# Query maxima of 12 of 32 attention units carried by an accumulating DMA, with a new order table: a hand-ordered attention and feed-forward kernel

## Chip, cores and metric

The kernel runs on one core of a Trainium2 chip. The metric is device time in microseconds (us). The engines are PE (matrix products), DVE (VectorE), ACT (ScalarE), POOL (GpSimd) and SP (SyncE, which here issues most DMAs).

## The reference

The reference is a kernelised attention over 8 batches × 8 heads, sequence 576, head dimension 64, 128 features, and a feed-forward block with a cosine behind it:

```
def phi(x):
    proj = np.einsum('bhsd,df->bhsf', x, w_phi)
    proj = proj - np.max(np.abs(proj), axis=-1, keepdims=True)
    return np.concatenate([np.exp(proj), np.exp(-proj)], axis=-1)
q_p, k_p = phi(q), phi(k)
kv  = np.einsum('bhsf,bhsd->bhfd', k_p, v)
z   = np.sum(k_p, axis=2)
num = np.einsum('bhsf,bhfd->bhsd', q_p, kv)
den = np.einsum('bhsf,bhf->bhs', q_p, z)[..., None] + 1e-06
attn_out = num / den

x = attn_out as (4608, 512)
h = x @ w_in            # 512 x 2048
g = h * np.cos(h)
out = g @ w_out         # 2048 x 512
```

The step the change is about is `proj - max|proj|` for the queries: every token has one maximum over the 128 features.

## The kernel before

The host hands over `q` and `k` transposed, two heads to a unit, so there are 32 units. For each, `attention(u)` writes down the steps of its work; `convert` and `fold` write down the preparation of `w_in` and `w_out`, `visit` the feed-forward block for single blocks of tokens, `visit_two` for two blocks together. Nothing is issued while these functions run. Each piece is a `Step` with its engine, a cost, what it depends on and which buffers it takes and uses. `plan()` (L260) then walks one hand-kept list, `ORDER` (L88), of 3852 step numbers, assigns PSUM banks and the two value buffers, and the steps are issued in that order. So each engine works strictly in the order in which its steps stand in the list, and so does SP's queue of DMA issues: a load that waits for a buffer holds up every load behind it.

Projections of a unit's queries have the feature index on the 128 partitions and the 2 × 576 tokens along the free axis, in `pq` (ACT copies them there from PSUM, `q_copy`, L583). The maximum over partitions is made in these steps:

- `q_red` (DVE, L589): a reduction with transposition inside blocks of 32×32 gives `m1`, with absolute values taken.
- `q_max` (DVE, L597, L598): the four groups of 32 partitions are brought down to one, `m3`.
- `q_spread` (POOL, L603): three copies put it back on the other three groups.
- `q_turn` (DVE, L607): a transposition of 128×1152 spreads every maximum over the partitions, into `bq`.
- `q_sub` (POOL, L611): four subtractions `pq - bq`, a quarter of the tokens each.
- `exp_q` (ACT, L682): the exponentials into `eq`, from which PE computes the numerators and denominators (`x_mm`, L755).

The keys have tokens on partitions, so that DVE takes their maximum directly (`k_max`, L656; `k_neg`, L659) and ACT subtracts it as a bias in the exponential (`exp_k`, L676). PE forms `kv` (L722, L728), ACT copies it (`kv_out`, L734), DVE divides (L767 to L785), SP stores the result to DRAM, `xs` and `xs_tail`.

In the feed-forward part `hi_of` and `lo_of` (L50 on ACT, L55 on DVE) split a tile into a rounded part and a rest, so that a product is three matmuls: L1023 to L1025 in `visit`, L1374 to L1376 in `visit_two`. `x` comes back by loads `x_raw<-xs` (L1116), parts and sums of `w_out` by `wo<-wo_parts` (L1351) and `wo<-wo_sums` (L1347), all on SP. The cosine waves are L981 to L1007 and L1296 to L1307, each an alternation of DVE and ACT. L398 to L423 are conversions of `w_in` and `w_out` on DVE.

Attention, conversions and the `visit`s share the first 535 us; the three `visit_two` fill the rest. The value buffers and the place of every step are set here:

```
elif b.ring == "v":
    b.slot, n_v = n_v, 1 - n_v
return [steps[i] for i in ORDER]
```

Of the kernel before, what the change touches and what calls it, by code (L numbers as in the profile page):

```python
# [17 lines left out]
P = 128  # L18
# [8 lines left out]
def phi_attention_then_cos_ffn(ctx: ExitStack, tc: tile.TileContext, qkT, vS, w_phi, w_in, w_out, out, out_t):  # L27
# [41 lines left out]
    class Step:  # L69
# [190 lines left out]
    def plan():  # L260
        place = {steps[x]: i for i, x in enumerate(ORDER)}
        owner = [None] * len(banks)
        n_v = 0

        def last(b):
            return -1 if b is None else max(place[v] for v in b.users)

        for x in (steps[i] for i in ORDER):
            for b in x.take:
# [4 lines left out]
                elif b.ring == "v":  # L274
                    b.slot, n_v = n_v, 1 - n_v
# [1318 lines left out]
```

## Time and profile before

| | |
|---|---|
| runs | 1010.91, 1015.84, 1015.05 us; median 1015.05 |
| profiled execution | 1013.98 us, its span 1012.3 us, 22252 instructions |
| mean granted clock of PE | 0.998 |
| busy | PE 991.7 us (98%), DVE 892.5 (88%), ACT 769.7 (76%), POOL 164.3 (16%) |
| DMA | 210.60 MB, mean 208 GB/s |
| chain that ended last, by engine | PE 77%, DVE 10%, DMA 7%, ACT 2%, issue 2%, POOL 1% |

The span is what the profiler recorded from the first instruction to the last; the profiled execution's own time is 1.7 us longer. Busy time is the time in which an engine has an instruction in work. A share of the whole span mixes stretches in which different engines are full, so the table is only where one begins. In rows of the trace, `PEclk` is TensorE's granted clock as a share of full speed, `SPq` is SP's queue, and an arrow in brackets names what ended an engine's idle time.

### The profile page before, as it was taken

How to read it: one execution, taken by the hardware profiler on the slowest of the kernel's cores; microseconds unless marked ns; L12 is line 12 of the kernel's file. 1: busy time of each engine (PE TensorE's matmuls, PEld its weight loads, DVE VectorE, ACT ScalarE, POOL GpSimd, SP SyncE). 2: the span in 40 equal slices, each digit the busy share in tenths (PEclk: the TensorE clock that was granted, in tenths of full speed). 3: DMA queues.
4: the chain of work that ended last, by engine and by line, in shares of the span. 5: the costliest groups of instructions: out<-in, count | busy, mean ns of one | idle time of the engine just before them, and what ended most of it. 6: DMA issues, size and time to landing. Idle time of an engine off the chain costs nothing.

```text
span 1012.3 us, 22252 instructions
## 1 busy us (share of the span) xinstructions
PE 991.7 (98%) x8586; PEld 803.5 (79%) x8586; DVE 892.5 (88%) x1590; ACT 769.7 (76%) x1575; POOL 164.3 (16%) x231
## 2 busy tenths in 40 slices
PE   9999999999999999999989999899999999999997
PEld 6778878888788878788767888688888888888886
DVE  6999999999899999899989979798778998787984
ACT  6899999688878988899997666557565766665653
POOL 4544130121112123333550000000000000000000
PEclk9999999999999999999999999999999999999999
DMA  6667776456676578888767663447546575375364
GB/s 233 187 192 229 240 214 206 138 188 233 208 236 205 212 227 286 282 283 254 232 198 247 222 217 141 158 165 270 200 151 228 171 219 206 126 247 203 98 225 145
DMA packets 104569, 210.60 MB, mean 208 GB/s; under 512 B 21392, under 2 KB 52240, under 8 KB 100880
## 3 DMA queue, kind: packets, MB, share of 16 engines
q1 hardware_dynamic: 104320, 209.13, 62.4%
q8 instruction: 67, 1.10, 0.4%
q14 instruction: 38, 0.31, 0.1%
q10 hardware_dynamic: 144, 0.07, 0.0%
HBM read 152.54 MB, written 56.62 MB: 207 GB/s over the span
## 4 chain that ended last, share of the span: by engine, by line
PE 77%; DVE 10%; DMA 7%; ACT 2%; issue 2%; POOL 1%; SPq 1%; DVEq 0%; POOLq 0%; ACTq 0%
PE bank L1201 23%; PE bank L974 9%; PE bank L1374 7%; PE bank L1376 7%; PE bank L1375 7%; PE bank L1023 3%; PE bank L1025 3%; PE bank L1024 3%; PE bank L755 3%; PE bank L722 3%; PE bank L618 2%; PE bank L572 2%; DMA vs<-vS 1%; DVE mk L656 1%; DVE m L589 1%
## 5 line engine op out<-in xcount | busy, mean ns | idle before, releaser
L1374 PE MATMUL bank<-gh,wo 128*128 128x512 f32 x336 | 132.4, 394 | 6.0 <-DMA wo<-wo_parts 4.2
L676 ACT ACTIVATE ek<-bank,mk 128x128 f32<-128x128 f32 x464 | 132.9, 486 | 4.2 <-DVE mk L659 2.3
L611 POOL TENSOR_TENSOR pq<-pq,bq 128x288 f32<-128x288 f32 x128 | 120.1, 969 | 97.9 <-DVE bq L607 72.0
L1376 PE MATMUL bank<-gl,wo 128*128 128x512 f32 x336 | 132.0, 393 | 0.0
L1375 PE MATMUL bank<-gh,wo 128*128 128x512 f32 x336 | 131.7, 392 | 0.0
L682 ACT ACTIVATE eq<-pq 128x576 f32<-128x576 f32 x128 | 83.8, 793 | 6.2 <-POOL pq L611 4.8
L603 POOL COPY m<-m 32x36 f32<-32x36 f32 x96 | 43.4, 452 | 268.3 <-DVE m L598 254.2
L1298 ACT ACTIVATE g<-hs 128x512 int32<-128x512 f32 x96 | 59.6, 626 | 34.7 <-DVE hs L1217 33.6
L1304 ACT ACTIVATE g<-g,halfpi 128x512 f32<-128x512 f32 x96 | 66.9, 717 | 24.8 <-DVE g L1301 24.6
L1201 PE MATMUL bank<-x_eq,wi 128*128 128x512 f32 x216 | 84.8, 393 | 0.1
L1211 ACT ACTIVATE hs<-bank 128x512 f32<-128x512 f32 x96 | 56.0, 591 | 35.6 <-PE bank L1201 25.2
L1374 PEld LDWEIGHTS bank<-gh,wo 128*128 128x128 f32 x336 | 63.4, 189 | 21.5 <-issue 6.7
L1023 PE MATMUL bank<-wo,gh 128*128 128x512 f32 x192 | 77.2, 402 | 0.6 <-ACT pq L583 0.4
L1201 PE MATMUL bank<-xh_t,wi 128*128 128x512 f32 x192 | 76.0, 396 | 0.3 <-ACT hs L1211 0.3
L1025 PE MATMUL bank<-wo,gl 128*128 128x512 f32 x192 | 75.3, 392 | 0.3 <-DVE gl L55 0.2
L1024 PE MATMUL bank<-wo,gh 128*128 128x512 f32 x192 | 74.9, 390 | 0.0
L1376 PEld LDWEIGHTS bank<-gl,wo 128*128 128x128 f32 x336 | 63.5, 189 | 14.2
L1301 DVE SCALAR_TENSOR_TENSOR g<-g,hs 128x512 f32<-128x512 int32 x96 | 64.9, 686 | 11.1 <-ACT g L1298 10.8
L1375 PEld LDWEIGHTS bank<-gh,wo 128*128 128x128 f32 x336 | 63.6, 189 | 13.8
L755 PEld LDWEIGHTS bank<-kv,eq 128*64 128x64 f32 x2048 | 64.9, 138 | 11.8 <-issue 3.4
L755 PE MATMUL bank<-kv,eq 128*64 128x65 f32 x2048 | 70.8, 223 | 1.3 <-DVE rb L781 0.5
L722 PE MATMUL bank<-vs,ek 128*64 128x65 f32 x2048 | 67.4, 223 | 1.9 <-ACT ek L676 1.5
(170 smaller groups left out, 2517.2 us busy)
## 6 DMA issues: line engine op xcount, KB each, us to landing
wi<-wi_parts SPq DMA_DIRECT2D x18, 1792.0 KB, 7.6
wo<-wo_sums SPq DMA_DIRECT2D x20, 1024.0 KB, 6.1
qk<-qkT SPq DMA_DIRECT2D x31, 640.0 KB, 5.3
x_raw<-xs SPq DMA_DIRECT2D x47, 256.0 KB, 4.0
wo<-wo_parts SPq DMA_DIRECT2D x22, 512.0 KB, 8.8
vs<-vS SPq DMA_DIRECT2D x32, 325.0 KB, 4.9
wi_raw<-w_in SPq DMA_DIRECT2D x8, 1024.0 KB, 6.3
wo_raw<-w_out SPq DMA_DIRECT2D x8, 1024.0 KB, 6.6
```

The source lines that it names most:

```text
L611: qeng.tensor_tensor(out=d["pq"][:, c], in0=d["pq"][:, c], in1=d["bq"][:, c], op=ALU.subtract)
L676: ACT.activation(out=e[:, g, s * P:(s + 1) * P], in_=pk[:, g, :], func=AF.Exp, scale=1.0 - 2.0 * s, bias=d["lk" if s == 0 else "mk", i][:, ...
L722: PE.matmul(out=acc[c:c + 64, n, i, :], lhsT=e[:, s, P * n + c:P * n + c + 64], rhs=vs[b["v"].slot][:, 2 * s + i, :], start=(s == 0 and i ...
L755: PE.matmul(out=ps[64 * h:64 * h + 64, 65 * t:65 * t + 65], lhsT=d["eq", i][:, n, c:c + 64], rhs=d["kv"][:, 2 * n + i, :], start=h not in ...
L974: PE.matmul(out=bank(b), lhsT=w[:, part, 2 * r + kt // 2, kt % 2 * P:(kt % 2 + 1) * P], rhs=d.get(("from", kt), d)[x, kt], start=(k == 0), ...
L1023: PE.matmul(out=a, lhsT=gh[:, t], rhs=w[:, 0, r], start=first, stop=False)
L1024: PE.matmul(out=a, lhsT=gh[:, t], rhs=w[:, 1, r], start=False, stop=False)
L1025: PE.matmul(out=a, lhsT=gl[:, t], rhs=w[:, 0, r], start=False, stop=last)
L1201: PE.matmul(out=bank(bank_b), lhsT=w[:, part, block, j * P:(j + 1) * P], rhs=d[x, name, j], start=start and k == 0, stop=k == 5, skip_grou ...
L1374: PE.matmul(out=a, lhsT=w_of(0, m), rhs=n["gh"], start=first, stop=False, skip_group_check=True)
L1375: PE.matmul(out=a, lhsT=w_of(1, m), rhs=n["gh"], start=False, stop=False, skip_group_check=True)
L1376: PE.matmul(out=a, lhsT=w_of(0, m), rhs=n["gl"], start=False, stop=True, skip_group_check=True)
```

## The change

For units 10 to 21 the query maxima take another way. `q_red` writes the negated maxima, with the tokens of a block read side by side. `q_least` takes minima of them into a constant tile `least` of 32×64 and transposes it into `m4`, in which a partition holds the 32 tokens of a block. `q_put` writes `m4` to DRAM as one row of 1152 numbers, `most_q[u]`. `q_add` reads that row for all 128 partitions at once and adds it to `pq` in the DMA itself (`accum_op=ALU.add`). Both DMAs are issued by POOL. `q_spread`, `q_turn` and the four `q_sub` do not exist for these units; the other 20 units keep them. Value buffers go to the one that is freed first in the order, instead of alternating. `ORDER` is written anew: 3804 numbers in place of 3852. DVE has 12 steps fewer, POOL 36 fewer; PE, ACT and SP have as many as before.

```diff
     def plan():
         place = {steps[x]: i for i, x in enumerate(ORDER)}
         owner = [None] * len(banks)
-        n_v = 0
+        owner_v = [None] * len(vs)
...
                 elif b.ring == "v":
-                    b.slot, n_v = n_v, 1 - n_v
+                    b.slot = min(range(len(vs)), key=lambda i: last(owner_v[i]))
+                    assert last(owner_v[b.slot]) < place[x]
+                    owner_v[b.slot] = b
...
+    least = const.tile([32, 64], F32, name="least")
+    POOL.memset(least, 0.0)
...
+    Q_ADDED = range(10, 22)
...
+    most_q = dram.tile([NU, 2, 2 * NJ, 32], F32, name="most_q")
...
         def q_red(j):
+            if u in Q_ADDED:
+                DVE.tensor_reduce(out=d["m1"][:, 2 * j * NJ:2 * (j + 1) * NJ],
+                                  in_=d["pq"][:, j * S:(j + 1) * S].rearrange("p (b f) -> p b f", f=32), axis=AX.X,
+                                  op=ALU.max, apply_absolute_value=True, apply_transpose=True, negate=True)
+                return
...
+        def q_least():
+            m1 = d["m1"]
+            m2 = new("bq", [64, 4 * NJ], F32, "m2", "m2")
+            d["m4"] = new("bq", [32, 64], F32, "m4", "m4")
+            DVE.tensor_tensor(out=m2, in0=m1[0:64], in1=m1[64:128], op=ALU.min)
+            DVE.tensor_tensor(out=least.rearrange("p (j c) -> p j c", j=2)[:, :, 0:2 * NJ],
+                              in0=m2[0:32].rearrange("p (j c) -> p j c", j=2), in1=m2[32:64].rearrange("p (j c) -> p j c", j=2), op=ALU.min)
+            DVE.transpose(out=d["m4"], in_=least)
+        def q_put():
+            POOL.dma_start(out=most_q[u].rearrange("h j t -> j h t"), in_=d["m4"][0:2 * NJ].rearrange("j (h t) -> j h t", h=2))
+        def q_add():
+            most = most_q[u].rearrange("h j t -> (h j t)").unsqueeze(0).broadcast_to([P, 2 * S])
+            POOL.dma_start(out=d["pq"], in_=most, accum_op=ALU.add)
...
-        qm = Step("DVE", 0.41, q_max, reds, take=[b["bq"]], use=[b["pq"]], port=True, kind=phase + "q_max")
...
+        if u in Q_ADDED:
+            qm = Step("DVE", 0.58, q_least, reds, take=[b["bq"]], use=[b["pq"]], port=True, kind=phase + "q_max")
+            qm = Step("POOL", 0.9, q_put, [qm], use=[b["bq"]], kind=phase + "q_put")
+            qs = [Step("POOL", 0.9, q_add, [qm], use=[b["pq"]], kind=phase + "q_add")] * 4
+        else:
+            qm = Step("DVE", 0.41, q_max, reds, take=[b["bq"]], use=[b["pq"]], port=True, kind=phase + "q_max")
...
             eqs.append(Step("ACT", 1.15, lambda j=j: exp_q(j),
-                            qs[2 * j:2 * j + 2], take=[e], use=[b["pq"]],
+                            qs[2 * j:2 * j + 1] if u in Q_ADDED else qs[2 * j:2 * j + 2], take=[e], use=[b["pq"]],
...
     ORDER = [
-        0, 3, 42, 4, 5, 59, 7, 45, 44, 1, 6, 8, 9, 17, 18, 10, 19, 46, 21, 11, 48, 58, 1265, 47, 12, 62, 14, 23, 20, 22, 15, 2, 49, 25,
...
```

The order table moves steps everywhere. Three places matter for what follows. Lines behind the edit have moved: L1116, L1351 and L1347 before are L1145, L1380 and L1376 now; L50 and L55 stay; L676, L682 and L1004 are L705, L711 and L1033. In the rows, a name's number tells one buffer from the next, `x4` is a count of equal instructions.

The first place is SP's queue in the first `visit_two`, some 100 us after attention has ended: loads of `x` and of parts of `w_out`. Before:

```order
L1351 DMA wo_8266<-wo_parts_90 128x2x256 x4
L1116 DMA x_raw_8349<-xs_77 128x512
L1116 DMA x_raw_8442<-xs_77 128x512
L1351 DMA wo_8444<-wo_parts_90 128x2x512 x2
L1116 DMA x_raw_8468<-xs_77 128x512
L1347 DMA wo_8508<-wo_sums_99 128x2048
```

After:

```order
L1380 DMA wo_8253<-wo_parts_92 128x2x256 x4
L1145 DMA x_raw_8304<-xs_77 128x512
L1380 DMA wo_8379<-wo_parts_92 128x2x512 x2
L1145 DMA x_raw_8420<-xs_77 128x512
L1145 DMA x_raw_8422<-xs_77 128x512
L1376 DMA wo_8430<-wo_sums_101 128x2048
```

One load of `x_raw` that stood ahead of the load of `wo` (8444 before, 8379 now) stands behind it.

The second place is DVE at the same point. A load of `x_raw` takes a buffer of its ring of four, so it waits for that buffer's last reader: `x_raw_8442` for `xl_t3_8427`, `x_raw_8304` now for `xl_t1_8235`. The first matmuls with the new `wo` tile read `gh_8432` and `gl_8438` before, `gh_8385` and `gl_8387` now. Before:

```order
L55 TENSOR_TENSOR gl_8409<-g_wi_7690,gh_8382 128x512
L55 TENSOR_TENSOR gl_8411<-g_wi_7690,gh_8398 128x512
L1301 SCALAR_TENSOR_TENSOR g_8333<-g_8333,hs_8285 128x512
L55 TENSOR_TENSOR xl_t3_8427<-x_raw_8189,xh_t3_8426 128x512
L55 TENSOR_TENSOR gl_8438<-xt_t_8329,gh_8432 128x512
L1307 TENSOR_TENSOR x_raw_t_8440<-hs_8285,g_8333 128x512
```

After, the first and the last rows of the 19 that lead from the one to the other:

```order
L55 TENSOR_TENSOR xl_t1_8235<-x_raw_7737,xh_t1_8234 128x512
L1167 TENSOR_TENSOR x_raw_7821<-x_raw_8156,x_raw_7821 128x512
L1352 TENSOR_TENSOR xt_t_8297<-hs_8167,g_wi_7619 128x512
...
L1167 TENSOR_TENSOR x_raw_8304<-x_raw_8304,x_raw_8156 128x512
L55 TENSOR_TENSOR xl_t2_8357<-x_raw_8156,xh_t2_8356 128x512
L55 TENSOR_TENSOR gl_8387<-xt_t_8297,gh_8385 128x512
```

The last reader of the buffer and the operand of the next product stood next to each other; now 18 rows of DVE lead from the one to the other.

The third place is unit 10, the first that takes the new way. DVE after, from the minima on:

```order
L613 TENSOR_TENSOR m2_1778<-m1_1616 64x36
L614 TENSOR_TENSOR least_82<-m2_1778 32x2x18
L616 STREAM_TRANSPOSE m4_1779<-least_82 32x64
L401 SCALAR_TENSOR_TENSOR wo_t1_1702<-wo_raw_1389,wo_t0_1701 128x1024
L55 TENSOR_TENSOR gl_1796<-g_1394,gh_1773 128x512
L404 TENSOR_SCALAR wo_t0_1701<-wo_t1_1702 128x1024
L1029 SCALAR_TENSOR_TENSOR g_1769<-g_1769,hs_1768 128x512
L688 TENSOR_SCALAR mk_1610<-mk_1610 128x4
L423 TENSOR_TENSOR wo_t2_1703<-wo_raw_1389,wo_t0_1701 128x1024
L688 TENSOR_SCALAR mk_1754<-mk_1754 128x4
L1036 TENSOR_TENSOR g_1457<-hs_1456,g_1457 128x512
```

ACT after, from the first row that reads DVE's last one above to the exponentials of unit 10:

```order
L50 ACTIVATE gh_1816<-g_1457 128x512
L1033 ACTIVATE g_1769<-g_1769,halfpi_81 128x512
L705 ACT_TABLE_LOAD
L705 ACTIVATE ek_1870<-bank4_73,mk_1754 128x128 x8
L50 ACTIVATE gh_1883<-g_1769 128x512
L50 ACTIVATE xh_t1_1887<-x_raw_1794 128x512
L50 ACTIVATE xh_t3_1900<-x_raw_1814 128x512
L705 ACTIVATE ek_1914<-bank2_71,mk_1610 128x128 x8
L50 ACTIVATE xh_t4_1924<-x_raw_1818 128x512
L711 ACTIVATE eq_1929<-pq_1617 128x576 x2
```

Before, DVE had in this unit's place the turn, among other work:

```order
L597 TENSOR_TENSOR m2_1805<-m1_1711 64x36
L598 TENSOR_TENSOR m3_1806<-m2_1805 32x36
L767 TENSOR_SCALAR dn_1815<-bank5_74 128x4
...
L607 STREAM_TRANSPOSE bq_1841<-m3_1806 128x1152
```

Between the last row of the maxima on DVE and the exponentials that read `pq_1617` stand eight rows of DVE and, behind the last of these, nine entries of ACT.

## Rows read from the trace of the kernel before

**Rows 1.** Busy time by stretch: length, PE, PEld, DVE, ACT, POOL, PEclk, DMA share, GB/s.
```profile
0.00:100.00 100.00, 98.14 (x1617) 75.83 (x1619) 89.58 (x193) 85.57 (x194) 48.54 (x75) 1.00 0.65 208
100.00:450.00 350.00, 347.86 (x3418) 284.90 (x3416) 325.37 (x567) 304.75 (x641) 78.06 (x101) 1.00 0.69 226
450.00:550.00 100.00, 93.18 (x1611) 75.97 (x1608) 94.49 (x213) 93.82 (x250) 37.68 (x56) 1.00 0.74 233
550.00:1012.00 462.00, 452.57 (x1954) 366.81 (x1952) 383.07 (x620) 285.60 (x495) 0.00 (x0) 1.00 0.56 190
```
**Rows 2.** Waits of PE, 550 us to the end: total us, times, longest.
```profile
PE bank L1374 <- DMA wo<-wo_parts: 4.2, 1, 4.2
PE bank L1374 <- DMA wo<-wo_sums: 1.7, 1, 1.7
```
**Rows 3.** Timeline of PE, 635 to 645 us: start, duration, instruction, idle before.
```profile
635.40 0.39 PE L1376 MATMUL bank<-gl,wo 128*128 128x512 f32 x1
640.02 0.47 PE L1374 MATMUL bank<-gh,wo 128*128 128x512 f32 x1 [4.22 <-DMA wo<-wo_parts]
...
644.20 0.40 PE L1376 MATMUL bank<-gl,wo 128*128 128x512 f32 x1
```
**Rows 4.** Busy time by stretch, just behind that wait.
```profile
641.50:644.00 2.50, 2.50 (x7) 1.93 (x7) 0.86 (x2) 1.15 (x2) 0.00 (x0) 0.50 0.73 306
```
**Rows 5.** Timeline of all engines, 632.6 to 634.2 us, DVE and SP's queue.
```profile
632.71 0.68 DVE L55 TENSOR_TENSOR xl_t<-x_raw,xh_t 128x512 fp32r<-128x512 f32 x1
...
633.42 0.33 SPq L1116 DMA_DIRECT2D x_raw<-xs  x1
...
633.84 0.53 SPq L1351 DMA_DIRECT2D wo<-wo_parts  x1
```
**Rows 6.** Groups of instructions by line and shape: busy us, mean ns, idle before.
```profile
L607 DVE STREAM_TRANSPOSE bq<-m 128x1152 f32<-128x1152 f32 x32 | 43.8, 1369 | 3.7 <-POOL m L603 3.5
L611 POOL TENSOR_TENSOR pq<-pq,bq 128x288 f32<-128x288 f32 x128 | 120.1, 969 | 97.9 <-DVE bq L607 72.0 <-ACT ek L676 8.0 <-ACT pq L583 7.5
L676 ACT ACTIVATE ek<-bank,mk 128x128 f32<-128x128 f32 x464 | 132.9, 486 | 4.2 <-DVE mk L659 2.3 <-PE bank L728 1.6
L1004 ACT ACTIVATE g<-g,halfpi 128x512 f32<-128x512 f32 x48 | 33.7, 719 | 7.6 <-DVE g L1000 7.2
L1004 ACT ACT_TABLE_LOAD x15 | 19.2, 1283 | 0.2
L50 ACT ACTIVATE gh<-g 128x512 fp32r<-128x512 f32 x48 | 31.4, 656 | 7.5 <-DVE g L1007 5.9 <-DVE mk L659 1.6
L50 ACT ACTIVATE xh_t<-x_raw 128x512 fp32r<-128x512 f32 x24 | 15.7, 669 | 0.5 <-DVE x_raw L1138 0.5
L398 DVE SCALAR_TENSOR_TENSOR wo_t<-wo_raw,wo_t 128x1024 uint32<-128x1024 uint32 x8 | 9.7, 1215 | 0.1
L420 DVE TENSOR_TENSOR wo_t<-wo_raw,wo_t 128x1024 f32<-128x1024 uint32 x8 | 9.7, 1210 | 0.0
L55 DVE TENSOR_TENSOR gl<-g,gh 128x512 fp32r<-128x512 f32 x48 | 35.8, 748 | 1.7 <-ACT gh L50 1.5
L1000 DVE SCALAR_TENSOR_TENSOR g<-g,hs 128x512 f32<-128x512 int32 x48 | 33.9, 707 | 2.0 <-ACT hs L982 1.7
```
**Rows 7.** POOL's copies in `q_spread`: ns, least/median/most; then their group.
```profile
L603 POOL COPY m<-m x96: 206/210/2384, 9.1 to 525.4; 32x36 f32<-32x36 f32 x96
...
L603 POOL COPY m<-m 32x36 f32<-32x36 f32 x96 | 43.4, 452 | 268.3 <-DVE m L598 254.2 <-DVE dn L767 11.4
```
**Rows 8.** DMA issues: size, median us from issue to landing; last row least/median/most, L1351.
```profile
xs_tail<-xt SPq DMA_DIRECT2D x32, 32.0 KB, 3.9
wo_raw<-w_out SPq DMA_DIRECT2D x8, 1024.0 KB, 6.6
...
DMA to landing us min/median/max: 3.0/8.5/10.4
```
**Rows 9.** Busy time by stretch, ten us inside the end of attention.
```profile
510.00:520.00 10.00, 7.78 (x168) 6.13 (x164) 9.79 (x26) 9.57 (x33) 4.32 (x7) 1.00 0.86 251
```

More of the change, by code (lines that the diff above doesn't have):

```diff
@@ L631, in attention @@
                 for j in range(2)]
-        qm = Step("DVE", 0.41, q_max, reds, take=[b["bq"]], use=[b["pq"]], port=True, kind=phase + "q_max")
-        qm = Step("POOL", 0.45, q_spread, [qm], use=[b["bq"]], port=True, kind=phase + "q_spread")
-        qm = Step("DVE", 1.3, q_turn, [qm], use=[b["bq"]], kind=phase + "q_turn")
-        qs = [Step(qname, qcost, lambda j=j: q_sub(j), [qm], use=[b["pq"], b["bq"]], port=True, kind=phase + "q_sub") for j in range(4)]
+        if u in Q_ADDED:
[4 more added lines that the diff above has]
+            qm = Step("DVE", 0.41, q_max, reds, take=[b["bq"]], use=[b["pq"]], port=True, kind=phase + "q_max")
+            qm = Step("POOL", 0.45, q_spread, [qm], use=[b["bq"]], port=True, kind=phase + "q_spread")
+            qm = Step("DVE", 1.3, q_turn, [qm], use=[b["bq"]], kind=phase + "q_turn")
+            qs = [Step(qname, qcost, lambda j=j: q_sub(j), [qm], use=[b["pq"], b["bq"]], port=True, kind=phase + "q_sub") for j in range(4)]
         def k_mm(tail):
```

333 rows, old and new, of the table ORDER are left out of this document.

## The prediction, made before the result was known

> **What bounds the kernel now.** I read the busy time by stretch first [rows 1], because the change sits in one stretch (units 10 to 21 run between about 100 and 450 us) while its new order table moves work everywhere. The reader is to see that PE is the bound in each stretch, and how little it idles: 100.00 − 98.14 = 1.9 us up to 100 us, 350.00 − 347.86 = 2.1 us from 100 to 450, 6.8 us from 450 to 550 and 462.00 − 452.57 = 9.4 us after that. No instruction of PE's is removed, so the whole change can give back at most the sum, 20.2 us, and whatever the clock loses at a stall. Where the edited units lie there are 2.1 us to win, although 12 units lose a 1.37 us turn on DVE: DVE is busy there for 325.37 of 350 us, but PE does not wait for it.
>
> Second, what PE waits for in the last stretch [rows 2]: one wait of 4.2 us for a load of `wo` from `wo_parts`, one of 1.7 us for a load from `wo_sums`. The rest of the 9.4 us, some 3.5, is mostly the end of the program, where nothing is left to run.
>
> Third, the longer of those waits in PE's timeline [rows 3]. Matmuls start every 0.23 us (452.57 / 1954 in [rows 1]); after the one at 635.40 the next starts at 640.02 instead of 635.63, so 4.39 us go. Then the granted clock falls: 0.50 between 641.5 and 644 [rows 4], which is the lower level of 1.2 and 2.4 GHz, after a stop of PE. Eleven matmuls start from 640.02 up to the one at 644.20, 4.18 us where 11 × 0.23 = 2.5 would do: 1.7 us more. **The stall costs 4.4 + 1.7 = 6.1 us.**
>
> Its cause is in the rows of all engines just before [rows 5]. On SP a load of `x_raw` (L1116) goes out at 633.42, right behind the DVE instruction that reads its buffer last (`xl_t`, 632.71 + 0.68 = 633.39). The `wo` load (L1351) goes out behind it at 633.84, and PE gets its tile at 640.02, 6.2 us later. So the `wo` load was not waiting for its own buffer as the last thing: it was queued on SP behind another load that waited for DVE.
>
> **The change, part by part.**
> *Order on SP, late (A).* In the new order the corresponding `wo` load, `wo_8379`, still stands behind an `x_raw` load. But that one's buffer is read last by `xl_t1_8235`, which stands 18 DVE instructions ahead of `gl_8387`, the operand of the first matmuls with the new tile; before, `xl_t3_8427` stood directly ahead of `gl_8438`. At 0.68 us apiece [rows 5] that is 12 us of DVE work. Counted on PE, 48 matmuls stand between that release and the first use, 48 × 0.23 = 11 us, where 6 stood before; 6.2 us are needed. The stall and its clock loss go: −6.1, with bounds −6.1 and 0, since something else may be late in its place.
>
> *The `wo_sums` load (A2).* 29 matmuls of cover in place of 25: 4 × 0.23 = −0.9 of the 1.7 us [rows 2]; bounds −1.7 and 0. The other late loads have at least 29 matmuls (6.7 us) of cover in the new order, and the next late thing is this one.
>
> *DVE work that goes (B).* Twelve turns of 1.369 us [rows 6] leave; a transposition of 32×64 comes, by elements per partition 64 / 1152 of that or little more, taken as 0.15. The difference is 12 × 1.2 = 14.6 us of DVE, in a stretch where PE idles for 2.1. I take −1.0, bounds −2.1 and 0. The 48 subtractions of 0.969 us [rows 6] and 36 copies of POOL's leave an engine that is busy for 78 of 350 us; they are priced at nothing but as a part of the chain below.
>
> *Chain to the exponential (F).* Before, from the maxima to the last subtraction: 3 × 0.452 + 1.369 + 4 × 0.969 = 6.6 us (means of [rows 6, 7]; the 0.452 is the 43.4 us of the 96 copies divided). After: transposition 0.15, DMA of 4.6 KB out to DRAM, DMA of 590 KB back with accumulation. Neither DMA is in the trace. Nearest small one: 32 KB to DRAM, 3.9 us to landing; nearest large one by bytes moved (590 KB read and 590 KB written, 1.18 MB): 1024 KB, 6.6 us [rows 8]. With two issues on POOL of 0.33 to 0.53 like SP's [rows 5], the chain is an estimated 0.15 + 3.9 + 6.6 + 0.9 = 11.6 us, 5 us longer than before.
> What hides it: in the new order of unit 10, DVE has after `m4` the rows L401 1.215, `gl` 0.748, L1029 0.707, L423 1.210 and `g_1457` about 0.7, together 4.6 us; ACT's `gh_1816` reads `g_1457`, so that it starts behind these, and from it ACT has 0.656 + 0.719 + 1.283 + 8 × 0.486 + 0.656 + 3 × 0.669 + 8 × 0.486 = 13.1 us until `exp_q` (durations of the same lines before, [rows 6]). That is 17.7 us. The same count gives 17.4 for unit 21, the shortest, and for the others 19.6, 20.6, 21.3, 21.6, 23.8, 24.3, 25.2, 25.6, 26.1 and 35.9. 11.6 < 17.4: hidden, 0. If the cover is gone, ACT, which runs in order, stands still with `ek` and `gh` behind it, and PE waits for these. Behind `q_put` and `q_add` on POOL stands only work of other units; `q_add` holds POOL for the 3.9 us of the first DMA, twelve times, in a stretch where POOL idles for 272 us.
> The bounds of the chain: below, the two transfers at the least that a row of such loads shows, 3.0 us each [rows 8], 6.9 us in all; above, each issue held as long as POOL's longest copy, 2.384 us [rows 7], and each DMA as long as the longest landing, 10.4 us [rows 8]: 0.15 + 4.8 + 20.8 = 25.7 us. I stay by the nearest rows.
> One row bears on the upper end: a 32×36 copy on POOL takes 206 ns at the least, 210 in the median and 2384 at worst [rows 7], so something holds POOL now and then. The Trainium skill, "SBUF — State Buffer", section "SBUF: two separate sides", has a box on this: the descriptors of a DMA issued from GpSimd are written by GpSimd itself, which is locked out while VectorE runs a two-port operation; a DMA from ScalarE's or SyncE's queue is spared. By that rule these two DMAs are the ones of the kernel that DVE can hold up, and at the copy's 2.4 us for each the chain would be 0.15 + 3.9 + 6.6 + 4.8 = 15.5 us, still under 17.4 but with 2 us in hand, where my sum has 6.
>
> *DMA traffic (G).* 12 × 1.18 MB = 14.2 MB in 350 us are 40 GB/s on top of 226, at a share of 0.69 [rows 1]: about 0.81. At 510 to 520 us the DMA engines already stand at 0.86, and there DVE (9.79 of 10) and ACT (9.57) are the full ones [rows 9]. I take 0, bounds 0 and +2.
>
> *ACT and PE switches (D, E).* The order has two more ACT table loads, 2 × 1.283 = 2.6 us [rows 6], in a stretch where ACT idles for 45 us: 0, at most +2.6. PE changes its tile shape 4 times more: 0, at most 4 × 0.23 = +0.9.
>
> *450 to 550 us (C).* Units 22 to 31 keep their operations. DVE and ACT are 94 to 98% busy there [rows 1, 9], and the new order puts some 4 us more of DVE's work into the last 100 us of PE's attention: 0, bounds −6.8 (all idle time gone) and +4.
> *Value buffers by first freed.* With two buffers it only changes which one a load takes; the loads' places stand in the order. 0.
>
> **Sum:** −6.1 − 0.9 − 1.0 = −8.0. Against the profiled execution's 1013.98 this is 1006.0; the median of the runs shown, 1015.05, stands 1.1 above it, so I say **1007**.
>
> **Rivals.**
> *More.* DVE, 14.6 us lighter, gets ahead and the 6.8 us between 450 and 550 go too: 1000. For it: DVE is the fullest engine there. Against it: the saving lies before that stretch, and the order moves other work in. Chance 0.12.
> *Another late load.* The order table has some 400 transfers on SP; if one of them, or DVE's part of an operand, is late by 6 us where the old one was, or 450 to 550 takes its +4, the gain is used up: 1012 to 1017. For it: PE has 2% of idle time and one misplaced wait cost 6.1 us. Against it: the counts above. Chance 0.22.
> *The chain shows (slower).* Beyond 17.4 us `exp_q` waits, first in unit 21, then in others; by the twelve covers above the waits add up to 8.7 us at a chain of 21, where they eat the 8 us gained, to 26 at 24 and to 39.8 at 25.7. With half of 39.8 reaching PE, since ACT has idle time to make some of it good: 1007 + 19.9 = 1027. For it: POOL's worst copy and the longest landing; accumulation is in no row. Against it: it needs both DMAs near the worst rows. Chance 0.11.
>
> **How the numbers follow.** Forecast 0.55. A measurement of this kernel tells about 0.5%, 5.1 us, from no change, so faster means below 1010. Of the forecast and *more*, 0.67 together, 0.05 falls above that: faster 0.62. Same: that 0.05 and 0.21 of the second and third cases. Slower: 0.12, from the chain and the far end of the late load. The range goes from 998, a little below *more*, to 1017, the far end of the late load; the chain's end beyond it is left out.
>
> **What would show it.** PE's wait for `wo<-wo_parts` and the granted clock of 0.50 behind it are gone; PE's idle time from 550 us on falls from 9.4 to about 4.3 (4.2 and 0.9 less); the two new DMAs land 3 to 8 us after issue and ACT's `eq` lines (L711) do not list `pq` by DMA among their releasers; DVE is busy for about 15 us less. I am wrong if `eq` waits for DMA (the chain), if PE's waits after 550 us name another load of 4 us or more, or if the idle time from 450 to 550 moves by more than 4 us.

## The result, and the profile after

The changed kernel took 1002.73 us in the median (1000.93 to 1003.70), beside 1014.08 before (the 1015.05 of the prediction with a fourth run): a ratio of 0.989, 95% interval 0.986 to 0.992, so 8 to 14 us less. Measured again later beside the experiments it was 1002.74, beside 1012.22: 0.992, interval 0.989 to 0.994. The forecast was 1007, with a range of 998 to 1017. The ratios of the experiments below go to medians of the kernel before that were measured beside them, 1011.9 to 1012.5; "above the changed kernel" means above 1002.74.

The profiled execution after took 1003.56 us, its span 1001.9: 10.4 less than before. Busy time by stretch of the changed kernel, with the columns of [rows 1]:

```profile
0.00:100.00 100.00, 97.61 (x1640) 76.24 (x1641) 89.38 (x191) 85.48 (x192) 49.64 (x75) 1.00 0.63 200
100.00:450.00 350.00, 346.81 (x3356) 283.96 (x3356) 301.09 (x567) 306.35 (x637) 29.48 (x41) 1.00 0.80 246
450.00:550.00 100.00, 95.92 (x1659) 79.66 (x1655) 96.43 (x216) 97.67 (x261) 39.92 (x58) 1.00 0.79 248
550.00:1001.90 451.90, 447.58 (x1942) 363.45 (x1940) 380.89 (x619) 286.00 (x492) 0.00 (x0) 1.00 0.57 192
600.00:650.00 50.00, 50.00 (x218) 40.49 (x217) 47.19 (x78) 37.17 (x66) 0.00 (x0) 1.00 0.50 168
```

PE idles for 4.3 us from 550 on, where it was 9.4, and the last row, which takes in the place of the long wait before, has PE busy without a gap at full clock. From 450 to 550 it idles for 4.1 where it was 6.8. From 100 to 450, where the edited units lie, it idles for **3.2 us, not 2.1**: nothing was won there, although DVE is 24 us less busy.

PE's waits from 550 us to the end, after, all of them:

```profile
PE bank L1403 <- DVE o_t L1477: 0.2, 1, 0.2
```

Both waits of [rows 2] are gone, 4.2 and 1.7 us. SP's queue after, at the place of [rows 5]:

```profile
622.33 0.33 SPq L1145 DMA_DIRECT2D x_raw<-xs  x1
623.12 1.17 SPq L1380 DMA_DIRECT2D wo<-wo_parts  x2
```

The `wo` load goes out at 623.12 instead of 633.84, again behind a load of `x_raw`, which now waits for a DVE instruction that stands earlier. The second wait of [rows 2] in PE's timeline before:

```profile
995.30 0.39 PE L1376 MATMUL bank<-gl,wo 128*128 128x512 f32 x1
997.40 0.47 PE L1374 MATMUL bank<-gh,wo 128*128 128x512 f32 x1 [1.72 <-DMA wo<-wo_sums]
```

So by the trace the late part gave 4.4 + 1.7 (the clock) + 1.9 (997.40 − 995.30 − 0.23, the second wait with its whole gap) = 8.0 of the 10.4 us. Outside these two waits PE's idle time is nearly what it was (20.2 − 5.9 = 14.3 us before, 14.0 after); where the other 2.4 us went is not shown.

### The profile page after: what moved, and what is told of

Its sections match the earlier page's. It is cut to its first block, busy times and chain, and to the rows that moved or that the text cites. A ratio compares the mean times of both kernels' runs of the same rounds, so it can differ in the third digit from the quotient of the medians.

```text
span 1001.9 us, 22210 instructions
## 1 busy us (share of the span) xinstructions
PE 987.9 (99%) x8586; PEld 803.3 (80%) x8586; DVE 867.8 (87%) x1590; ACT 775.5 (77%) x1577; POOL 119.0 (12%) x172
## 4 chain that ended last, share of the span: by engine, by line
PE 80%; DVE 8%; ACT 5%; DMA 5%; issue 1%; SPq 1%; POOL 0%; DVEq 0%; ACTq 0%; POOLq 0%
PE bank L1230 23%; PE bank L1003 11%; PE bank L1403 8%; PE bank L1405 8%; PE bank L1404 8%; PE bank L1052 4%; PE bank L1054 4%; PE bank L1053 4%; PE bank L784 3%; PE bank L751 3%; ACT ek L705 2%; PE bank L576 2%; DMA vs<-vS 1%; DVE mk L685 1%; DVE m L598 1%
## 5 line engine op out<-in xcount | busy, mean ns | idle before, releaser
L705 ACT ACTIVATE ek<-bank,mk 128x128 f32<-128x128 f32 x464 | 131.6, 448 | 3.0 <-DVE mk L688 2.8
L711 ACT ACTIVATE eq<-pq 128x576 f32<-128x576 f32 x128 | 82.7, 754 | 4.8 <-POOL pq L636 4.8
L1333 ACT ACTIVATE g<-g,halfpi 128x512 f32<-128x512 f32 x96 | 67.1, 715 | 12.9 <-DVE g L1330 12.5
L636 POOL TENSOR_TENSOR pq<-pq,bq 128x288 f32<-128x288 f32 x80 | 71.8, 928 | 36.7 <-DVE bq L632 29.5
L1403 PEld LDWEIGHTS bank<-gh,wo 128*128 128x128 f32 x336 | 63.1, 188 | 14.3 <-DVE o_t L1477 0.7
L751 PEld LDWEIGHTS bank<-vs,ek 128*64 128x64 f32 x2048 | 62.7, 138 | 6.0 <-issue 2.5
```

Of the source, the lines that this page charges most:

```text
L705: ACT.activation(out=e[:, g, s * P:(s + 1) * P], in_=pk[:, g, :], func=AF.Exp, scale=1.0 - 2.0 * s, bias=d["lk" if s == 0 else "mk", i][:, ...
L711: ACT.activation(out=e[:, s, :], in_=d["pq"][:, j * S:(j + 1) * S], func=AF.Exp, scale=1.0 - 2.0 * s)
L751: PE.matmul(out=acc[c:c + 64, n, i, :], lhsT=e[:, s, P * n + c:P * n + c + 64], rhs=vs[b["v"].slot][:, 2 * s + i, :], start=(s == 0 and i ...
L1403: PE.matmul(out=a, lhsT=w_of(0, m), rhs=n["gh"], start=first, stop=False, skip_group_check=True)
```

## The chain of DMAs, as it ran

Unit 10 in the changed kernel: the transposition on DVE, the two DMAs on POOL, and ACT. Columns are start, duration, instruction, idle time before it.

```profile
106.13 0.23 DVE L616 STREAM_TRANSPOSE m<-least 32x64 f32<-32x64 f32 x1
```
```profile
106.69 0.78 POOL L619 DMA_DIRECT2D most_q<-m  x1 [2.98 <-DVE m L616]
111.01 0.92 POOL L623 DMA_DIRECT2D pq<-most_q  x1 [3.53 <-DMA most_q<-m]
```
```profile
112.96 1.28 ACT L705 ACT_TABLE_LOAD   x1
114.26 2.17 ACT L705 ACTIVATE ek<-bank,mk 128x128 f32<-128x128 f32 x8
116.27 0.68 ACT L50 ACTIVATE gh<-g 128x512 fp32r<-128x512 f32 x1
116.80 1.20 ACT L50 ACTIVATE xh_t<-x_raw 128x512 fp32r<-128x512 f32 x2
117.84 2.22 ACT L705 ACTIVATE ek<-bank,mk 128x128 f32<-128x128 f32 x8
119.84 0.74 ACT L50 ACTIVATE xh_t<-x_raw 128x512 fp32r<-128x512 f32 x1
120.36 1.36 ACT L711 ACTIVATE eq<-pq 128x576 f32<-128x576 f32 x2
```

The second DMA (L623) of this unit, from its issue to its landing:

```profile
DMA to landing us min/median/max: 9.2/9.2/9.2
```

It landed at 120.25, and `eq` began at 120.36: hidden, by 0.11 us. Over the 12 units the chain, from the end of the transposition to the landing, took 9.3 to 15.7 us, 12.5 in the mean (forecast 11.6); the margin was 0.1 us in unit 10, 1.2 in unit 21, 2.2 in unit 20 and 6 to 14 in the others. What ACT's `eq` lines waited for after:

```profile
  POOL pq L636: 4.8, 7
```

Only subtractions of the units that kept the old way are named, no DMA.

## Experiments: the late loads

**One step moved in the kernel before.** Step 2514 is the `wo` load that PE waited for, 2760 the `x_raw` load ahead of it.

```diff
+    def ahead(a, b):
+        ORDER.remove(a)
+        ORDER.insert(ORDER.index(b), a)
+    ahead(2514, 2760)
```

> The kernel before with one step moved on SP: the wo load from wo_parts that PE waited 4.2 us for is issued ahead of the x_raw load instead of behind it; nothing else changes. Theory (the late loads make most of the gain): PE's wait for wo<-wo_parts and the granted clock of 0.50 behind it go, the 1.7 us wait for wo<-wo_sums stays: 6.1 us less than before, 1008. Rival (the gain comes from DVE's lighter load in attention, and the late wait would only move to another load): within 1.5 us of before.

Measured: 1004.84 us, ratio **0.993**, interval 0.992 to 0.995 (4.7 to 8.6 us less). PE's waits from 550 us to the end:

```profile
PE bank L1378 <- DMA wo<-wo_sums: 1.7, 1, 1.7
```

The long wait is gone and nothing took its place, without any change of the queries' way. The theory's size holds; the rival falls.

**The second load too**, step 3821, put ahead of step 3834, the one that is used after it:

```diff
+    ahead(2514, 2760)
+    ahead(3821, 3834)
```

> The kernel before, old way and old order, with two steps moved on SP: the wo load from wo_parts ahead of the x_raw load, as in the first experiment, and near the end the wo load from wo_sums that PE waited 1.7 us for ahead of the one that is used after it. Theory (most of the gain is two loads that were late): both late waits gone, 6.1 + 1.9 = 8.0 us less than before, ratio 0.992, within 3 us of the changed kernel. Rival (a load that is moved ahead makes the next one late): the ratio of the first experiment, 0.993, or higher.

Measured: 1009.91, ratio 0.999, interval 0.997 to 1.001. Worse than the one move alone. PE's longest wait and ACT behind it:

```profile
PE bank L1379 <- ACT o_t L1443: 3.9, 1, 3.9
```
```profile
988.06 0.60 ACT L1443 ACTIVATE o_t<-bank 128x512 f32<-128x512 f32 x1 [4.97 <-DMA out_t<-o_t]
```

And the stretch behind that wait, with the columns of [rows 1]:

```profile
989.40:996.10 6.70, 5.49 (x13) 4.37 (x14) 3.59 (x6) 2.31 (x5) 0.00 (x0) 0.50 0.21 78
```

The load that was pushed one place back has to wait for its buffer, and now stands ahead of the stores of `out_t`; ACT needs those to be over before it may write `o_t` again, and PE needs ACT; behind PE's stop the granted clock was 0.50 for 6.7 us. It is the disorder of the first stall once more, made by the move, as the rival foresaw. So the two loads were exchanged in their places instead, the stores staying between them:

```diff
+    ahead(2514, 2760)
+    at = ORDER.index(3834), ORDER.index(3821)
+    ORDER[at[0]], ORDER[at[1]] = 3821, 3834
```

> The kernel before with the first experiment's move, and the last two wo loads of wo_sums exchanged in their places on SP, so that the stores of out_t between them stay behind one load that waits for nothing and ahead of the one that waits. Theory (two late loads are most of the gain; moving one load ahead of the stores only put the stores behind a wait): both waits gone and no wait for o_t, 8 us less than before, ratio 0.992 or a little less. Rival (that end of the program is bound otherwise): the first experiment's 0.993 or higher.

Measured: 1004.23, ratio **0.992**, interval 0.989 to 0.995; from 550 us on the trace names no wait of PE at all. Beside it the changed kernel as it is:

> The changed kernel as it is, beside the others on the same chip. All theories: ratio 0.986 to 0.992; its distance to the kernel with two loads moved is what the new way and the rest of the new order bring: some 2 to 3 us by the profiles, 0 by the theory that the late loads are all of it.

Measured: 1002.74, ratio **0.992**, interval 0.989 to 0.994. The old way in the old order with two loads in other places is as fast as the changed kernel, within what these runs can tell (some 0.4%, 4 us). What the second move adds to the first alone, 0.993 to 0.992, lies inside the intervals; that its wait is gone is shown by the trace.

## Experiments: the way of the maxima

**The old way in the new order.**

```diff
+    for x in ((417, 424), (452, 432), (487, 1628), (522, 1264), (557, 1771), (592, 1869), (627, 628), (662, 1911), (697, 757), (732, 723), (767, 718), (802, 831)):
+        ahead(*x)
...
-            if u in Q_ADDED:
+            if False:
...
-            qm = Step("DVE", 0.58, q_least, reds, ...
-            qm = Step("POOL", 0.9, q_put, [qm], ...
-            qs = [Step("POOL", 0.9, q_add, [qm], ...
+            qm = Step("DVE", 0.58, lambda: (q_max(), q_spread()), reds, ...
+            qm = Step("POOL", 0.9, lambda: (q_turn(), [q_sub(j) for j in range(4)]), [qm], ...
+            qs = [Step("POOL", 0.9, lambda: None, [qm], ...
```

> The changed kernel in its new order, but units 10 to 21 make their maxima as before: three copies on POOL, the turn on DVE, four subtractions on POOL, placed four DVE steps behind the maxima. DVE has some 15 us more to do between 100 and 450 us. Theory (late loads): the late part stays without waits, PE's idle time from 100 to 450 us grows by 0 to 4 us: 1003 to 1007. Rival (the accumulating DMA makes the gain by relieving DVE): most of the 11 us goes, 1010 or more.

Measured: 1021.37, ratio **1.010**, interval 1.008 to 1.012: 18.6 us above the changed kernel. Its stretch of 100 to 450 us, and what ACT waited for there:

```profile
100.00:450.00 350.00, 335.87 (x2986) 270.59 (x2986) 318.38 (x528) 289.22 (x585) 78.88 (x93) 1.00 0.63 209
```
```profile
ACT gh L50 <- DVE g L1041: 10.6, 12, 3.6
```

PE idles for 14.1 us where the changed kernel has 3.2, and ACT's wait for DVE's `g` is 10.6 us where it was 3.0. My theory was wrong by far here: it priced DVE's work by what PE idled in the *old* order, but the new order is laid out for a lighter DVE, and put back into it in these places the work costs 18.6 us. Other places for it were not tried. The rival, that the relief makes the gain, foresaw the direction, yet not that it is worse than before by 9.5 us, nor that the old way needs only two moves to be as fast.

**The new way in the old order.** In the kernel before, `q_least`, `q_put` and `q_add` stand in the places of `q_max`, `q_spread` and `q_turn` for units 10 to 21; the `q_sub` steps are empty.

```diff
...
+        added = u in Q_ADDED
+        qm = Step("DVE", 0.41, q_least if added else q_max, ...
+        qm = Step("POOL", 0.45, q_put if added else q_spread, ...
+        qm = Step("DVE", 1.3, q_add if added else q_turn, ...
+        qs = [Step(qname, qcost, lambda j=j: None if added else q_sub(j), ...
```

> The kernel before in its old order, but units 10 to 21 send their maxima through DRAM and the accumulating DMA: the first DMA stands where POOL's copies stood, the second where DVE's turn stood. In the old order the time from the maxima to the exponentials was 10.9, 7.6, 11.9, 11.7, 10.9 and 9.9 us in units 10, 11 and 18 to 21, and the chain of DMAs took 13.9, 9.8, 10.6, 15.7, 13.8 and 13.9 us in them in the changed kernel: 16 us of waits on ACT. Theory (the order gives the cover and the late gain): 2 to 8 us more than before, 1016 to 1022, with both late waits still there. Rival (the relief of DVE makes the gain): 3 to 6 us less than before.

Measured: 1020.48, ratio **1.009**, interval 1.007 to 1.011, 7 to 11 us more than before. Waits of ACT for the whole run, one row of them, and of PE from 550 us on:

```profile
ACT eq L708 <- DMA pq<-most_q: 13.5, 5, 3.8
```
```profile
PE bank L1400 <- DMA wo<-wo_parts: 3.7, 1, 3.7
PE bank L1400 <- DMA wo<-wo_sums: 1.0, 1, 1.0
```

The mechanism is as foreseen, 13.5 us of ACT's waits, five of them, where 16 were worked out, and both late waits are there; the time is at the upper end or a little above. Neither half of the change, placed like this, is a gain by itself.

**The most that taking the work away can bring in the old order.** This kernel leaves out the copies, the turn and the subtractions of units 10 to 21.

```diff
+        gone = u in range(10, 22)
+        qm = Step("POOL", 0.45, lambda: None if gone else q_spread(), ...
+        qm = Step("DVE", 1.3, lambda: None if gone else q_turn(), ...
+        qs = [Step(qname, qcost, lambda j=j: None if gone else q_sub(j), ...
```

> The kernel before in its old order, leaving out the copies, the turn and the subtractions of units 10 to 21, so that their queries' exponentials take values without the maxima subtracted. DVE has 16.4 us less to do and POOL some 60, and there is no chain of DMAs. It shows the most that taking this work away can bring in the old order; the two late loads stay. Theory (PE idles 2.1 us between 100 and 450 us, so little is to be had there): 0 to 3 us less than before. Rival (relief of DVE and POOL is worth as much as adding it cost in the new order, 4.2 us for the turns and 13.5 for the subtractions): 8 us or more less.

Measured: 1010.31, ratio 0.998, interval 0.996 to 0.999: 2.2 us less in the median. Its stretch beside [rows 1]:

```profile
100.00:450.00 350.00, 348.70 (x3486) 286.71 (x3484) 302.68 (x561) 306.43 (x645) 11.98 (x18) 1.00 0.69 227
```

DVE is busy for 302.7 us in place of 325.4 and POOL for 12 in place of 78, and PE idles for 1.3 in place of 2.1. PE's waits from 550 us to the end, which were to stay as they were:

```profile
PE bank L1375 <- DMA wo<-wo_parts: 2.5, 1, 2.5
PE bank L1375 <- DVE gl L55: 2.0, 1, 2.0
```

They add up to 4.5 us where [rows 2] has 5.9, so not all of the 2.2 us need come from the stretch itself. The step of the prediction that took DVE's saving by PE's idle time (−1, at most −2.1) holds; the rival, 8 us or more, falls.

**The chain made longer**: two more copies from DRAM to DRAM.

```diff
+    hops = [dram.tile([NU, 2, 2 * NJ, 32], F32, name=f"hop{n}") for n in range(2)]
...
         def q_add():
-            most = most_q[u].rearrange("h j t -> (h j t)")...
+            for n in range(2):
+                POOL.dma_start(out=hops[n][u], in_=(hops[n - 1] if n else most_q)[u])
+            most = hops[1][u].rearrange("h j t -> (h j t)")...
```

> The changed kernel with the row of maxima copied twice more from DRAM to DRAM between the first DMA and the accumulating one, so that the chain is 4 to 10 us longer in each of the 12 units. The exponentials began 0.1, 2.2 and 1.2 us after the landing in units 10, 20 and 21 and 6 to 14 us after it in the others. Theory (the cover is used up in some units): ACT waits for pq by DMA, some 20 us in all, and 4 to 15 us more than the changed kernel: 1007 to 1018. Rival (ACT's idle time takes it in, the chain does not matter at this length): within 1.5 us of the changed kernel.

Measured: 1027.10, ratio **1.015**, interval 1.012 to 1.018, some 24 us above the changed kernel where 4 to 15 were expected; the runs lie between 1020.49 and 1032.67, and the profiled execution is the longest of them. ACT's wait over the whole run; PE's longest wait from 100 to 560 us; and a stretch of the profiled execution:

```profile
ACT eq L714 <- DMA pq<-hop: 23.0, 5, 8.1
```
```profile
PE bank L754 <- ACT ek L708: 7.6, 1, 7.6
```
```profile
450.00:500.00 50.00, 42.35 (x713) 35.53 (x712) 39.17 (x89) 41.28 (x113) 13.93 (x18) 0.90 0.77 245
```

ACT's waits are near the 20 us worked out, but they pass on more than whole (the span is 1031.0 us, 29 above the changed kernel's): PE stops for up to 7.6 us, and the granted clock of whole stretches is below 1, 0.90 in the row, which the expectation had not counted. So the cover of 14 us in unit 10 is a real limit, and the rival of the chain a real one: the kernel stands close to it.

## Experiments: turns or subtractions

Busy time by engine in the kernel with the old way in the new order:

```profile
PE 994.4 (98%) x8586; PEld 804.6 (79%) x8586; DVE 902.2 (88%) x1590; ACT 776.2 (76%) x1577; POOL 174.0 (17%) x232
```

In the changed kernel DVE was busy for 867.8 us. That is 34.4 less, where the prediction has 14.6 for 12 turns less the transpositions. (The 25.6 in the expectation below leaves out what lies behind the first 1001 us.) So two kernels added one kind of work each, for nothing, to the changed kernel.

```diff
+        def idle_turn():
+            d["bq"] = new("bq", [P, 2 * S], F32, "bq")
+            DVE.transpose(out=d["bq"], in_=wphi[:, 0:4 * NJ].unsqueeze(2).broadcast_to([P, 4 * NJ, 32]))
+        def idle_sub():
+            d["bq"] = new("bq", [P, 2 * S], F32, "bq")
+            x = wphi[:, 0:72].unsqueeze(1).broadcast_to([P, 4, 72])
+            for j in range(4):
+                POOL.tensor_tensor(out=d["bq"][:, j * HALF:(j + 1) * HALF].rearrange("p (a b) -> p a b", a=4), in0=x, in1=x, op=ALU.subtract)
...
-            qs = [Step("POOL", 0.9, q_add, [qm], use=[b["pq"]], kind=phase + "q_add")] * 4
+            qs = [Step("POOL", 0.9, lambda: (q_add(), idle_turn()), [qm], use=[b["pq"]], kind=phase + "q_add")] * 4
```

The second kernel has `idle_sub` in place of `idle_turn` in the last line.

> The changed kernel with 12 turns of 128x1152 on DVE added, one in each of units 10 to 21 behind the accumulating DMA's issue; nobody reads them. DVE gets 12 x 1.37 = 16.4 us back, POOL nothing. The kernel with the old way in the new order was some 18 us slower than the changed one, and DVE's busy time there was 25.6 us above the changed kernel's, not 14.6. Theory A (the new order has no room for DVE's turns): 8 to 16 us more than the changed kernel, 1011 to 1019. Theory B (POOL's subtractions make DVE's own instructions longer, and that is the larger part): at most 5 us more, DVE busy by 16 us more.

Measured: 1006.90, ratio 0.995, interval 0.993 to 0.997: 4.2 us above the changed kernel, with DVE busy for 882.4 us, 14.6 more.

> The changed kernel with 48 subtractions of 128x288 on POOL added, four in each of units 10 to 21 behind the accumulating DMA's issue, into a buffer that nobody reads. POOL gets some 45 us back, DVE no instruction. Theory A (DVE's turns are what the new order has no room for): within 2 us of the changed kernel. Theory B (POOL's work makes DVE's instructions longer): DVE's busy time grows by some 10 us without one instruction more, and the time by 4 to 10 us.

Measured: 1016.21, ratio 1.005, interval 1.003 to 1.007: **13.5 us above** the changed kernel, with no instruction more on DVE, which was busy for 891.4 us, 23.6 more. The two together are 17.7, close to the 18.6 of the old way in the new order. The chain of DMAs is not what the subtractions held up: ACT's `eq` lines wait here too only for subtractions of the units that kept the old way, and no longer than in the changed kernel (4.8 us).

```profile
  POOL pq L646: 4.9, 7
```

One of DVE's groups, its durations in ns (least/median/most): before, with the turns added, and with the subtractions added.

```profile
L55 DVE TENSOR_TENSOR gl<-g,gh x48: 649/684/1296, 98.2 to 470.5; 128x512 fp32r<-128x512 f32 x48
```
```profile
L55 DVE TENSOR_TENSOR gl<-g,gh x48: 630/683/693, 97.1 to 473.6; 128x512 fp32r<-128x512 f32 x48
```
```profile
L55 DVE TENSOR_TENSOR gl<-g,gh x48: 629/682/3387, 96.5 to 481.1; 128x512 fp32r<-128x512 f32 x48
```

And the longest of them, DVE and POOL in the kernel with the subtractions added:

```profile
334.18 3.39 DVE L55 TENSOR_TENSOR gl<-g,gh 128x512 fp32r<-128x512 f32 x1 [0.76 <-ACT gh L50]
```
```profile
334.17 2.84 POOL L633 TENSOR_TENSOR bq<-wphi 128x288 f32<-128x288 f32 x4
```

DVE's instruction, which alone takes 0.68 us, began 0.01 us after POOL's first subtraction and ended at 337.57, 0.56 us after POOL's fourth (334.17 + 2.84 = 337.01): it got going when the four were about over. Five of the twelve added groups of four held one DVE instruction to 2.8 to 3.4 us in this way. Theory B holds in kind, and both its sizes were too small (some 10 us of DVE's busy time, 4 to 10 of the run).

The busy time that DVE lost with the change is 892.5 − 867.8 = 24.7 us. By durations, the turns less the transpositions are 12 × (1.37 − 0.23) = 13.7 us. The DVE instructions that took over 100 ns longer than the median of their kind all ran beside a POOL subtraction: 35 of them before, 16.4 us too long in all, and 9 after, 2.5 us. (Durations overlap a little, so that the parts add up to more than 24.7.) None of those before was more than 0.67 us too long, so that the added subtractions, whose longest holds are some four times that, show the cause and not the price in the kernel before.

**Value buffers in turn again**, in the changed kernel.

```diff
-                    b.slot = min(range(len(vs)), key=lambda i: last(owner_v[i]))
+                    b.slot, n_v = n_v, 1 - n_v
```

> The changed kernel with the two value buffers taken in turn again instead of by first freed. All theories: the loads stand in the same places, within 1.5 us of the changed kernel; if a value load now waits for a buffer, PE names a wait for vs of over 1 us and the time is 2 to 5 us longer.

Measured: 1009.08, ratio 0.997, interval 0.995 to 0.999, about 6 us above the changed kernel, where 2 to 5 were expected with such a wait; PE names a wait for `vs`:

```profile
PE bank L749 <- DMA vs<-vS: 1.9, 1, 1.9
```

In the new order the values of units 5, 18 and 19 are loaded ahead of the last product that reads those of units 4, 16 and 18. Taken in turn, they go into the same buffers, so that these units' `kv` is formed in part from the other unit's values. The first-freed rule is therefore not a matter of taste: the new order needs it, which the prediction, where the rule only changed which buffer a load takes, did not see. That the rule costs nothing was not tried apart.

## Why the prediction was right

The sum of −8.0 us stands beside 11.4 and 9.5 measured (1014.08 − 1002.73, 1012.22 − 1002.74). Its main term was right; 1.0 of the difference is A2, and no run shows where the rest comes from.

- **The late wait (A, −6.1).** Right in place and size. The one move alone gave 0.993, 4.7 to 8.6 us, and the trace of the changed kernel has neither the wait nor the low clock.
- **The `wo_sums` load (A2, −0.9).** Right in direction, too small: the whole 1.9 us went. I counted four matmuls more of cover; the load after went out at 980.98 and landed in 7.2 us, as long as before (7.0), and PE did not wait for it. In the old order that wait is 1.7 us in two traces, 1.0 in the one with the new way, and not named in the one with the work left out.
- **DVE's saving (B, −1.0).** Not shown in its stretch: PE idles for 3.2 us from 100 to 450 in the changed kernel, 2.8 when it was measured again, and for 2.1 before. But the kernels with one load moved, two moved and two exchanged, which have the old way and the old order in that stretch, idle for 0.6, 2.6 and 1.1. In this order, the changed kernel's second trace last:

```profile
100.00:450.00 350.00, 349.36 (x3524) 287.92 (x3520) 328.09 (x574) 307.78 (x647) 78.57 (x101) 1.00 0.69 228
100.00:450.00 350.00, 347.40 (x3442) 285.92 (x3439) 327.04 (x572) 306.26 (x643) 78.50 (x101) 1.00 0.68 226
100.00:450.00 350.00, 348.93 (x3477) 286.86 (x3477) 328.93 (x576) 307.65 (x646) 79.56 (x102) 1.00 0.68 227
100.00:450.00 350.00, 347.19 (x3409) 285.23 (x3409) 301.98 (x571) 307.09 (x641) 29.90 (x42) 1.00 0.80 247
```

A microsecond either way in that stretch, and the 0.8 us of the kernel with the work left out, are within this scatter. The saving itself was 24.7 us, not 14.6, because I counted DVE's own instructions and not what POOL's cost it. Leaving the work out brought 2.2 us in the old order, about the bound I had given.
- **450 to 550 us (C, 0).** PE's idle time there fell by 2.7 us, inside the bounds of −6.8 and +4. Six traces in the old order show 4.1 to 6.8 us there, six in the new order (the one with the longer chain left out) 4.0 to 4.3. That the fall comes from the new order is likely by this, but was not tried apart.
- **The chain (F, 0).** Hidden, as I said, but I was lucky in the margin. The chain was 12.5 us in the mean where I had 11.6, and 13.9 in unit 10 (120.25 − 106.36); the cover in unit 10 was 120.36 − 106.36 = 14.0 us where I had 17.7. The failed term is "8 × 0.486": the mean of 486 ns is the duration of one instruction, and they overlap. Eight take 2.2 us in the rows above, not 3.9. The group's busy time by its count says so too, 132.9 / 464 = 0.286 us [rows 6]. Had I divided, two times 1.7 us less would have put the cover near 14. The shortest cover was unit 10's, not unit 21's.
- **DMA traffic (G, 0), switches (D, E, 0).** The share of the DMA engines from 100 to 450 us is 0.80, as I had it (0.81), at 246 GB/s and not 266: the profile counts 7.1 MB more, not 14.2. The table loads and PE's shape switches were not tried apart.
- **The rule of the Trainium skill.** I weighed it at "SBUF — State Buffer", section "SBUF: two separate sides", for DVE holding up POOL's descriptors. By these traces the time of the first DMA goes with the load of the DMA engines. In the changed kernel, the busy time over the first DMA's way in four units, and in the last two rows over the accumulating one's in units 14 and 16 (columns as in [rows 1]):

```profile
120.10:121.90 1.80, 1.80 (x48) 1.44 (x48) 1.55 (x4) 1.80 (x4) 0.63 (x1) 1.00 0.07 18
215.20:216.90 1.70, 1.70 (x9) 1.42 (x8) 1.63 (x3) 1.70 (x8) 0.62 (x1) 1.00 0.02 3
191.40:196.40 5.00, 5.00 (x28) 3.96 (x28) 5.00 (x9) 4.12 (x8) 0.62 (x1) 1.00 0.98 349
265.90:271.10 5.20, 5.20 (x24) 4.00 (x23) 2.89 (x7) 5.02 (x13) 0.59 (x1) 1.00 1.00 343
...
218.10:227.40 9.30, 9.30 (x43) 7.71 (x43) 6.53 (x11) 9.28 (x20) 0.35 (x1) 1.00 0.66 177
305.40:310.00 4.60, 4.60 (x23) 3.26 (x23) 2.74 (x4) 3.52 (x6) 0.29 (x1) 1.00 0.80 175
```

With the DMA engines at a share of 0.02 and 0.07 the 4.6 KB landed in 1.7 us, though DVE was busy for most of it; at 0.98 and 1.00 they took 5.0 and 5.2, in the last with DVE half idle. The accumulating DMA does not follow the load in this way: it took 9.9 us at 0.66 and 5.2 at 0.80, and why is open. The rows tell when DVE was busy, not which of its instructions take both ports, so they do not put the rule itself to the test. The same section of the Trainium skill says what I passed over: the port pair that GpSimd and VectorE share is an exclusive lock, and whichever starts first, a GpSimd instruction that reads SBUF or a VectorE instruction with two inputs from SBUF, holds it for the whole instruction. The 3.39 us above agree and go further: POOL began 0.01 us earlier, and not one but four of its instructions passed before DVE got in.

What the change is worth, then: by the runs, two loads in other places give as much as the whole of it. The accumulating DMA by itself costs 8.6 us in an order not made for it, and in the order made for it the chain is covered. Whether it is worth anything over the old way with the two loads mended is open: the medians are 1002.74 and 1004.23, and these runs do not tell 4 us apart. So is an order that is laid out afresh for the old way: it was not tried.

## What to carry to other kernels

When a kernel is bound by one engine at 98%, look first at which single waits hold the other 2%: here one load, queued behind another that waited for DVE, was 6 of the 11 us, and moving one number in the list gave them back. A table of order and the work it was made for belong together: each half alone was 8.6 and 9.5 us slower than before, so an edit tried without its order (or an order without its edit) says little about the edit. And cover that is counted in instructions is to be taken from a group's busy time divided by its count, not from the mean duration of one, which on ACT was 1.7 times as long.

## What the runs showed of the hardware that was not expected

- Four POOL subtractions of 128×288 in a row held a DVE instruction with two SBUF operands for about all of their 2.84 us, so that it took 3.39 us instead of 0.68. Whether a turn is held in the same way is not shown: none of the 32 before ran beside a subtraction.
- A DMA of 4.6 KB issued by POOL took 1.7 to 1.9 us to land at a DMA share of 0.02 to 0.07 (three units) and 4.3 to 5.4 at 0.97 to 1.00 (six); the accumulating one of 576 KB took 5.2 to 9.9.
- In the profiled execution of the kernel with the longer chain ACT's waits of 23 us came with 29 us more of the span: PE stood still for up to 7.6 us at a time, and its clock was granted at 0.90 over a stretch of 50 us.
